# A two-stage expert kernel on one core: the first product in chunks of 384 tokens instead of groups of 288

## The chip, the core and the metric

The kernel runs on one NeuronCore of a Trainium2 chip. The metric is the device time of one execution in microseconds (us); three executions of the kernel before were timed. The engines are PE (TensorE, the matmul array), DVE (VectorE), ACT (ScalarE), POOL (GpSimd) and SP (SyncE, which issues nearly all transfers). PE writes its results into banks of PSUM, of which this kernel names eight: two "A", three "B", one "C", one "M" and one "L".

## What is computed

The reference has three parts, one behind the other. All of it is single precision.

```python
attn_out = linear_attention(q, k, v, omega)       # 2 x 8 heads x 576 tokens x 64
x = attn_out.transpose(0, 2, 1, 3).reshape(1152, 512)
h = x @ w_in                                      # 1152 x 2048   "first product"
g = h / (1 + exp(-1.702 * h))
x = g @ w_out                                     # 1152 x 512    "y"
logits = x @ w_gate                               # 8 experts, capacity 288 tokens each
# top-1 routing; each token goes through its expert's relu(x @ w1) @ w2, times its gate weight
```

## The kernel before, in words

Every product is made of three single-pass matmuls, since an operand is held as a high part and a low part: `mm3` (lines 100 to 103) issues high x high (L101), high x low (L102) and low x high (L103). Small products that are not split run as fp32 in two passes, so that one call leaves two rows in the trace.

The 1152 tokens lie in four groups of GS = 288, G = 0 to 3. The weights of the first product come in NF = 16 blocks m of 128 columns. `do_h(G, m)` makes the first product of group G with block m: four contraction steps of three matmuls, each 288 columns wide, 12 in all; ACT then takes the sigmoid-gelu out of PSUM. For the even groups 0 and 2, ACT does this twice (`ghi`, `g32`) and DVE subtracts (`glo`, L660), and `do_y(G, m)` multiplies the parts by the second weights, again 12 matmuls of 288 columns. The odd groups 1 and 3 never get their y here: only their logits are needed, because a token of an odd group that wins a place in an expert is dealt with in a branch at the end (label "left", L1137 on), which this input does not enter. Their logits come from `g` times `wp`, the second weights already multiplied by the gate (`do_wg`, L520; `do_wp`, L533): `run_lg` collects four such `g` tiles and issues four fp32 matmuls with 8 output rows and 288 columns into one held bank "L" (L705), each in its own column group of the array, so that they run side by side.

The order of work is a list of slots, `seq`: each slot issues one `do_h`, and two slots later `do_consume` (y for even groups, logits for odd ones). In stage one the groups 0, 1 and 3 run over m, group 1 by 3 and group 3 by 5 blocks late; stage two is group 2 alone (16 slots from N2 = 48). Behind it (NSL = 64) stand the two experts, eight slots each, and `do_last`. Side work is hung on slots by number: the decoding of a weight block (`decode`: three DVE operations L260, L263, L266, for the second weights a DVE transpose L270, an ACT cast L276, and a subtraction L277 on POOL), `do_logits`, `do_pos` and `pick_slot`, which chooses an expert and starts its loads. A block is decoded up to six slots ahead of its use (`dlead=6`). The pace is set by `P` in line 16.

`mbank` (L93) hands out PSUM for small results: it alternates between the banks "L" and "M" as long as nothing stands in the list `held`, and gives "M" alone while something does. `do_lg` pops `held` after the last odd block. `do_last` (L937) writes the last group: it brings results back to token order by PE transposes into a bank from `mbank`, and DVE copies from there (`slot_rows` L1045, `chunk` L954; the last column block at L981 to L999). At the very end 76 tiny matmuls (L1009) stand on PE, and one transpose of a cleared tile.

Of the kernel before, what the change touches and what calls it, by code (L numbers as in the profile page):

```python
# [8 lines left out]
F32 = mybir.dt.float32  # L9
# [5 lines left out]
AX = mybir.AxisListType.X  # L15
P = dict(ahead=2, kvlag=2, t2=3, n=5, x=6, dec=(13, 16, 19, 22, 25, 28), tailstep=0.5, zero=26, w0=12, loadlag=10, pv=(0, 4), l1=3, l3=5, db=0.5, hpt=30, dmin=0.9, dc=1, dd=2, dlead=6, dpace=1.5, dv=6)

# [18 lines left out]
def linear_attention__moe__top1_moe_kernel(  # L36
# [26 lines left out]
    TT = 96  # L63
# [556 lines left out]

    L1, L3 = P["l1"], P["l3"]
# [21 lines left out]

    def do_h(G, m, full=False):
        tk = tokens(G)
        hi, lo = w_in(m)
        ps = bank("A", "h_ps")
        for c in range(KD):
            mark["hm"] = mm3(ps[:, :GS], hi[:, c], lo[:, c], x_hi[:, c, :, tk], x_lo[:, c, :, tk],
                             c == 0, c == KD - 1)  # L650
        if G % 2 and not full:
            g1 = gp.tile([128, GS], F32, tag="g1", name="g1", bufs=5)
            mark["a"] = nc.scalar.activation(g1, ps[:, :GS], ACTF.Gelu_apprx_sigmoid)  # L653
            gs[G, m] = g1
            return
        ghi, glo = parts_tile(G != 0)
        nc.scalar.activation(ghi, ps[:, :GS], ACTF.Gelu_apprx_sigmoid)  # L657
        g32 = gp.tile([128, GS], F32, tag="g1", name="g32", bufs=5)
        mark["a"] = nc.scalar.activation(g32, ps[:, :GS], ACTF.Gelu_apprx_sigmoid)  # L659
        mark["v"] = nc.vector.tensor_tensor(glo, g32, ghi.bitcast(F32), ALU.subtract)  # L660
        gs[G, m] = (ghi, glo)

# [17 lines left out]

    def do_lg(G, m):


        i = G - 1 + m % 2
        if i in lgq:
            run_lg()
        lgq[i] = (m, gs.pop((G, m)))
        if len(lgq) == 4 or (G, m) == (3, NF - 1):
            run_lg()
        if (G, m) == (3, NF - 1):  # L690
            held_t.append(gp.tile([128, GS], F32, tag="g1", name="lgt", bufs=5))
            nc.scalar.copy(rows_of(held_t[0]), in_order(held.pop()[:, :GS]))

    lgq, held_t, now = {}, [], [0]

    def run_lg():
        if not held:
            held.append(bank("L", "lgt_ps"))
            nc.vector.memset(held[0][:, :GS], 0.0)
        assert all(m in ready for m, _ in lgq.values()), (lgq, ready)  # L700
# [5 lines left out]
        lgq.clear()  # L706

    def do_consume(G, m):
        (do_lg if G % 2 else do_y)(G, m)

# [38 lines left out]
    def do_logits(G):  # L749
        if G % 2 == 0:  # L750
            ps = mbank("lg_ps")
            for c in range(KD):
                tk = tokens(G)
                nc.tensor.matmul(ps[:2 * E, :GS], wg[:, c].rearrange("p a e -> p (a e)"), x_hi[:, c, :, tk],
                                 start=(c == 0), stop=False)
                nc.tensor.matmul(ps[:E, :GS], wg[:, c, 0], x_lo[:, c, :, tk],
                                 start=False, stop=(c == KD - 1))
            t = gp.tile([2 * E, GS], F32, tag="g1", name="lgy", bufs=5)
            nc.scalar.copy(rows_of(t), in_order(ps[:2 * E, :GS]))
            n = 2 * E  # L760
        else:
            n = 64 if G == 1 else 128
            t = held_t[0]
        ps = mbank("lgr_ps")
        for j in range(TJ):
            nc.tensor.transpose(
                ps[:TT, j * n:(j + 1) * n], t[:n, j * TT:(j + 1) * TT], ident[:n, :n]
            )
        sl = slice(G * TJ, (G + 1) * TJ)
        a0 = 2 * (G == 3)  # L770
        parts = ps[:TT, :TJ * n].rearrange("p (j a e) -> p j e a", j=TJ, e=32 if G % 2 else E)
        nc.vector.tensor_reduce(lg[:, sl], parts[:, :, 0:E, a0:a0 + 2], AX, ALU.add)
        nc.vector.tensor_reduce(mx[:, sl], lg[:, sl], AX, ALU.max)
# [59 lines left out]
    def do_weights():  # L833
        n = NG * TJ
        d = small([TT, n, E], F32, "lgd")
# [101 lines left out]
    def do_last(wt):  # L937
# [65 lines left out]
        gone = gone[0:32, 0:32]  # L1003
        seen = gp.tile([32, 32], F32, tag="g1", name="seen", bufs=5)
# [68 lines left out]
    n0 = at_slot[0, NF - 1] + 3  # L1073
    n3 = at_slot[3, NF - 1] + 3
# [6 lines left out]
    N2 = NSL - NF  # L1081
# [55 lines left out]
    with tc.If(n_left > 0, label="left"):  # L1137
        n_odd = nc.values_load(st["odd"][0:1, 0:1], min_val=0, max_val=NP)
        n_g3 = nc.values_load(st["g3"][0:1, 0:1], min_val=0, max_val=NP)
        with tc.If(n_odd > 0):  # L1140
# [6 lines left out]
            for m in range(NF + 1):  # L1147
                if m < NF:
                    for i in (2 * m, 2 * m + 1):
                        for f in decode(*wseq[i], False):  # L1150
                            f()
                        if i + 3 < len(wseq):
                            load_w(*wseq[i + 3])
                    do_h(1, m, True)
                if m:
                    do_y(1, m - 1)
            with tc.If(n_g3 > 0):
                for m in range(NF + 1):
                    if m < NF:
                        do_h(3, m, True)  # L1160
                    if m:
# [66 lines left out]
```

## Time and profile before

| what | value |
|---|---|
| three executions | 322.84, 321.96, 322.47 us; median 322.47 us |
| the profiled execution | 322.61 us |
| its span in the trace | 320.8 us |
| PE busy | 314.4 us, 98% of the span |
| DVE, ACT, POOL busy | 198.2, 158.6, 45.2 us |
| attention with its tail | up to about 101 us |
| stage one (groups 0, 1, 3) | to about 206 us |
| stage two (group 2) | to about 256 us |
| the two experts and the end | to 320.8 us |

Matmuls are pipelined: the trace shows a 288-column matmul as 0.29 to 0.30 us long, but they start 0.13 us apart. What a matmul costs is therefore read from start to start, and a busy share of 98% does not say that the array works at its peak. The two columns of a timeline row are start and length in us.

### The profile page before, as it was taken

To read this page: it belongs to the slowest core of one execution; us is meant where nothing else is said; L and a number is where in the kernel's file an instruction comes from. 1 tells how busy PE (TensorE), PEld (TensorE's weight loads), DVE (VectorE), ACT (ScalarE), POOL (GpSimd) and SP (SyncE) were. 2 spreads that over 40 slices of the span, in tenths; PEclk is the share of its full clock that TensorE was granted. 3 is DMA by queue.
4 is the path that set the end of the run, shared out by engine and by line. 5 is a ranking of instruction groups with operands and counts; after the bars stand their busy time and mean duration, and the time that the engine had idled before them with its cause. 6 is when DMAs were issued, how large, how long until landed. Compare 5 with 4: busy or idle time off the path is not lost.

```text
span 320.8 us, 7172 instructions
## 1 busy us (share of the span) xinstructions
PE 314.4 (98%) x2844; PEld 301.7 (94%) x2844; DVE 198.2 (62%) x471; ACT 158.6 (49%) x424; POOL 45.2 (14%) x60
## 2 busy tenths in 40 slices
PE   8999999899999999999999999999999999999995
PEld 6999999789999999999999988989999999999995
DVE  5678888988679986686867324036624133567634
ACT  3788888779935434343434342234624233166411
POOL 3111211112000034333433200000000001010000
PEclk9999999999999999999999999999999999999998
DMA  7897672222003655444443000503510000276031
GB/s 210 254 329 176 196 218 65 67 68 66 2 24 109 204 192 167 164 132 133 143 145 109 0 2 2 196 2 131 138 61 3 0 2 0 72 253 200 19 93 44
DMA packets 32132, 35.23 MB, mean 110 GB/s; under 512 B 7553, under 2 KB 27137, under 8 KB 32097
## 3 DMA queue, kind: packets, MB, share of 16 engines
q1 hardware_dynamic: 31808, 34.69, 35.0%
q8 instruction: 23, 0.38, 0.5%
q14 instruction: 13, 0.10, 0.1%
q10 hardware_dynamic: 288, 0.07, 0.1%
HBM read 32.39 MB, written 2.36 MB: 108 GB/s over the span
## 4 chain that ended last, share of the span: by engine, by line
PE 92%; DVE 3%; ACT 1%; DMA 1%; issue 1%; SPq 0%; DVEq 0%; ACTq 0%
PE h_ps L101 14%; PE h_ps L103 13%; PE h_ps L102 13%; PE y L102 8%; PE y L101 8%; PE y L103 8%; PE kvp L367 4%; PE nps L392 4%; PE tp L310 3%; PE pj L101 3%; PE pj L103 2%; PE pj L102 2%; PE t L381 2%; PE lgt_ps L705 1%; PE wg_ps L520 1%; DMA qk_raw<-in_k_dram 1%
## 5 line engine op out<-in xcount | busy, mean ns | idle before, releaser
L660 DVE TENSOR_TENSOR glo<-g,ghi 128x288 fp32r<-128x288 f32 x27 | 13.2, 488 | 44.0 <-ACT g L659 44.0
L266 DVE SCALAR_TENSOR_TENSOR wf<-wraw,wf 128x512 int32<-128x512 int32 x32 | 28.6, 893 | 0.0
L653 ACT ACTIVATE g<-h_ps 128x288 f32<-128x288 f32 x32 | 13.1, 410 | 29.4 <-PE h_ps L103 26.0
L884 DVE TENSOR_TENSOR el<-eraw,eh 128x1024 fp32r<-128x1024 f32 x16 | 19.5, 1225 | 12.8 <-ACT eh L883 12.8
L336 DVE TENSOR_REDUCE nb<-pj 128x4 f32<-128x512 f32 (+1 forms) x40 | 25.1, 627 | 2.5 <-PE pj L103 2.3
L657 ACT ACTIVATE ghi<-h_ps 128x288 fp32r<-128x288 f32 x27 | 11.1, 410 | 28.3 <-PE h_ps L103 28.0
L101 PE MATMUL pj<-om_hi,xh 128*128 128x256 f32 x72 | 24.5, 340 | 0.2 <-ACT qp L349 0.2
L263 DVE SCALAR_TENSOR_TENSOR wf<-wraw,wf 128x512 int32<-128x512 int32 x32 | 23.1, 722 | 0.1
L883 ACT CAST eh<-eraw 128x1024 fp32r<-128x1024 f32 x16 | 16.6, 1046 | 13.0 <-issue 8.3
L349 ACT ACTIVATE qp<-pj,nb 128x128 f32<-128x128 f32 x72 | 21.7, 396 | 0.0
L102 PE MATMUL pj<-om_lo,xh 128*128 128x256 f32 x72 | 21.7, 302 | 0.0
L103 PE MATMUL pj<-om_hi,xl 128*128 128x256 f32 x72 | 21.6, 300 | 0.0
L349 ACT ACTIVATE kp<-pj,nb 128x128 f32<-128x128 f32 x72 | 21.4, 396 | 0.0
L367 PE MATMUL kvp<-vt,kp 128*128 128x65 f32 (+1 forms) x144 | 20.2, 270 | 0.1
L101 PE MATMUL h_ps<-x_hi,win0h 128*128 128x288 f32 x64 | 19.8, 310 | 0.0
L367 PEld LDWEIGHTS kvp<-vt,kp 128*128 128x128 f32 x144 | 18.9, 193 | 0.6 <-ACT kp L349 0.5
L313 ACT CAST xh<-tp 128x256 fp32r<-128x256 f32 (+1 forms) x40 | 14.8, 370 | 9.1 <-PE tp L310 8.9
L103 PE MATMUL h_ps<-x_hi,win0l 128*128 128x288 f32 x64 | 19.2, 300 | 0.1
L101 PE MATMUL h_ps<-x_hi,win1h 128*128 128x288 f32 x64 | 19.3, 301 | 0.0
L101 PE MATMUL h_ps<-x_hi,eh 128*128 128x288 f32 x64 | 19.2, 300 | 0.0
L320 DVE TENSOR_TENSOR xl<-tp,xh 128x256 fp32r<-128x256 f32 (+1 forms) x40 | 15.5, 389 | 5.9 <-ACT xh L313 5.7
L101 PE MATMUL h_ps<-x_hi,win2h 128*128 128x288 f32 x64 | 19.1, 299 | 0.0
(281 smaller groups left out, 1058.9 us busy)
## 6 DMA issues: line engine op xcount, KB each, us to landing
wraw<-in_moe_w_in_dram SPq DMA_DIRECT2D x16, 512.0 KB, 3.7
wraw<-in_moe_w_out_dram SPq DMA_DIRECT2D x16, 512.0 KB, 3.5
eraw<-in_moe_w_dram SPq DMA_DIRECT2D x16, 512.0 KB, 4.2
qk_raw<-in_v_dram SPq DMA_DIRECT2D x4, 512.0 KB, 5.1
qk_raw<-in_q_dram SPq DMA_DIRECT2D x4, 512.0 KB, 5.3
qk_raw<-in_k_dram SPq DMA_DIRECT2D x3, 512.0 KB, 5.3
out_dram<-zer SPq DMA_DIRECT2D x4, 192.0 KB, 4.3
out_dram<-base SPq DMA_DIRECT2D x3, 192.0 KB, 2.1
```

Of the source, the lines that this page charges most:

```text
L101: nc.tensor.matmul(o, lh, rh, start=start, stop=False)
L102: nc.tensor.matmul(o, lh, rl, start=False, stop=False)
L103: return nc.tensor.matmul(o, ll, rh, start=False, stop=stop)
L263: nc.vector.scalar_tensor_tensor(f, high, -0x40000000, f, ALU.bitwise_and, ALU.bitwise_or)
L266: nc.vector.scalar_tensor_tensor(f, low, 29, f, ALU.logical_shift_right, ALU.bitwise_or)
L313: nc.scalar.copy(xh[:, :n], tp[:, :n])
L320: nc.vector.tensor_tensor(xl[:, :n], tp[:, :n], xh[:, :n].bitcast(F32), ALU.subtract)
L336: mark["M", s] = nc.vector.tensor_reduce(nb[:, :nj], pj[:, :nj * M].rearrange("p (a m) -> p a m", m=M), AX, ALU.min)
L349: nc.scalar.activation(t[:, i], pj[:, i * M:(i + 1) * M], ACTF.Exp, bias=nb[:, i:i + 1], scale=-1.0)
L367: nc.tensor.matmul(ps[:, o:o + n], kp[:, i], vts[p][:, u, c0:c0 + n], start=(f == 0), stop=(f == NU - 1))
L883: nc.scalar.copy(hi, tv)
L884: nc.vector.tensor_tensor(lo, tv, hi.bitcast(F32), ALU.subtract)
```

## The change

The first product is cut otherwise. Instead of four groups of 288 there are three chunks of CS = 384 tokens: A is group 0 and the first 96 tokens of group 1, B is group 2 and the first 96 of group 3, C is what is left of the groups 1 and 3 (192 and 192). `do_h(X, m)` issues 12 matmuls of 384 columns. Out of the bank, ACT takes for A and B the two gelus of 288 columns as before and two more of 48 columns each (tile `ga`); for C one gelu of 384 columns (`gc`). The order is A and C interleaved (C four blocks late, `lc=4`) in stage one, and B alone in stage two; there are 48 slots instead of 64.

The logits of odd tokens are collected from these parts. `run_lg` no longer runs when four tiles are there but at given slots, takes the pairs of blocks that are ready, and issues fp32 matmuls of 48 columns (A, B) and 192 columns (C) into three regions of the held bank; `odd_out` copies the regions out. `held` is not popped any more. The logits of group 3 are finished four slots behind stage two. The tile `g1` has one buffer instead of five, decoding runs two to four slots ahead, and the 76 tiny matmuls are gone.

```diff
-P = dict(..., l1=3, l3=5, db=0.5, hpt=30, dmin=0.9, dc=1, dd=2, dlead=6, dpace=1.5, dv=6)
+P = dict(..., lc=4, db=0.5, hpt=30, dmin=0.75, dlead=2, dc=1, dd=1.5, dv=6)
...
+    CS = GS + TT
+    BH = TT // JF // 2
+    CB = (GI - TT // JF) * JF
     seq = []
-    for r in range(NF + L3):
-        seq += [(G, r - l) for G, l in ((0, 0), (1, L1), (3, L3)) if 0 <= r - l < NF]
-    at_slot = {gm: n for n, gm in enumerate(seq)}
-    seq += [(2, m) for m in range(NF)]
+    for r in range(NF + LC):
+        seq += [(X, r - l) for X, l in (("A", 0), ("C", LC)) if 0 <= r - l < NF]
+    at_slot = {xm: n for n, xm in enumerate(seq)}
+    seq += [("B", m) for m in range(NF)]
...
+    def chunk(t, c, X):
+        if X == "C":
+            return t[:, c].rearrange("p j (b i) -> p b j i", b=2)[:, :, :, GI + TT // JF:2 * GI]
+        o = 0 if X == "A" else 2 * GI
+        return t[:, c, :, o:o + CS // JF]
+    def do_h(X, m):
+        hi, lo = w_in(m)
+        ps = bank("A", "h_ps")
+        for c in range(KD):
+            mark["hm"] = mm3(ps[:, :CS], hi[:, c], lo[:, c], chunk(x_hi, c, X), chunk(x_lo, c, X),
                              c == 0, c == KD - 1)
+        if X == "C":
+            g = gp.tile([128, CS], F32, tag="gc", name="gc", bufs=3)
+            mark["a"] = nc.scalar.activation(g, ps[:, :CS], ACTF.Gelu_apprx_sigmoid)
+        else:
+            v = ps[:, :CS].rearrange("p (j i) -> p j i", j=JF)
+            h_parts("ACB".index(X), m, v[:, :, :GI])
+            g = gp.tile([128, TT], F32, tag="ga", name="ga", bufs=6)
+            for b in range(2):
+                nc.scalar.activation(g[:, b * TT // 2:(b + 1) * TT // 2].rearrange("p (j i) -> p j i", j=JF),
+                                     v[:, :, GI + b * BH:GI + (b + 1) * BH], ACTF.Gelu_apprx_sigmoid)
+        lgq.append((now[0], X, m, g))
...
     def run_lg():
         if not held:
             held.append(bank("L", "lgt_ps"))
-        with queued(mark["hm"]):
-            last = gates(sorted(wws), [wgq.pop(0)] if wgq else [])
+        todo = [q for q in lgq if q[0] < now[0] and q[2] in ready]
+        todo = [q for q in todo if any(o[1] == q[1] and o[2] == q[2] ^ 1 for o in todo)]
+        last = mark["hm"]
+        for X in "ACB":
+            at, w = region[X]
+            for b in range(2):
+                for q in todo:
+                    if q[1] != X:
+                        continue
+                    m, i = q[2], 2 * b + q[2] % 2
+                    with queued(last):
+                        nc.tensor.matmul(held[0][32 * i:32 * i + E, at:at + w], wp[:, m], q[3][:, b * w:(b + 1) * w],
+                                         start=((X == "B", i) not in opened), stop=(X != "A" and m >= NF - 2))
+        lgq[:] = [q for q in lgq if not any(q is t for t in todo)]
         with queued(last):
-            for i, (m, g) in sorted(lgq.items()):
-                nc.tensor.matmul(held[0][32 * i:32 * i + E, :GS], wp[:, m], g, start=(m < 2), stop=(m >= NF - 2))
+            gates(sorted(wws), [wgq.pop(0)] if wgq else [])
...
-        end = bank("A", "end_ps")
-        for _ in range(76):
-            tc.keep_in_program_order(nc.tensor.matmul(end[:32, 64:96], ones_bf[:, :32], ones_bf[:, :32], start=True, stop=True))
...
-        need = at_slot[0, m] + (0 if kd == "in" else 2) - P["dlead"]
-        n = max(int(i * P["dmin"]), min(need, int(i * P["dpace"])))
+        n = round(2 * max(i * P["dmin"], i - P["dlead"])) / 2
...
+    for n in [LC, *range(LC + 2, last_a + 1, 4), *range(last_a + 2, N2 + 1, 2)]:
+        slot(n, run_lg)
+    for n in range(N2 + 4, NSL + 1, 4):
+        slot(n, run_lg)
+    slot(N2 + 1, lambda: odd_out("C"))
+    slot(N2 + 1, lambda: odd_out("A"))
+    slot(NSL + 1, lambda: odd_out("B"))
...
-    slot(n3 + 1, lambda: do_logits(3))
+    slot(NSL + 4, lambda: do_logits(3))
```

Three places show what this does to PE's list of instructions.

The first is one of the breaks in stage one at which the gates and the odd logits are computed. Here is PE before (`h_ps` is the first product's bank, `g_2522` and the like are gelu tiles of the groups 1 and 3):

```order
L103 MATMUL h_ps<-x_hi,win2l 128x288
L533 MATMUL wg_ps<-back,ww 32x8 x8
L520 MATMUL wg_ps<-wt,wg_d 32x64 x16
L705 MATMUL lgt_ps<-g_2522,wp 8x288
L705 MATMUL lgt_ps<-g_2632,wp 8x288
L705 MATMUL lgt_ps<-g_2575,wp 8x288
L705 MATMUL lgt_ps<-g_2653,wp 8x288
L101 MATMUL h_ps<-x_hi,win2h 128x288
```

And here is PE in the changed program, at such a break (`ga`: four calls for two blocks of chunk A; `gc`: four for two of C):

```order
L103 MATMUL y_1698<-ghi,wout3l 128x288
L726 MATMUL lgt_ps<-ga,wp 8x48 x4
L726 MATMUL lgt_ps<-gc,wp 8x192 x4
L533 MATMUL wg_ps<-back,ww 32x8 x8
L520 MATMUL wg_ps<-wt,wg_d 32x64 x16
L101 MATMUL h_ps<-x_hi,win2h 128x384
```

The logits now stand ahead of the gate products, as eight narrower calls instead of four, and the first product around them is 384 columns wide. Behind the attention there are ten such breaks before: one with L520 alone, six with all three lines (two logit calls in the first of them, four in the others), one with L533 and logits, two with logits alone (four calls and two). In the changed program there are eleven up to the start of stage two: one with L520 alone, one with L533 and `ga`, one with L520 and `ga`, one with `gc` and both gate lines, four like the piece above, and three with the last logits (with L533; `ga` and `gc`; `gc` alone). Four more are new in stage two.

The second place is stage two, where PE before runs from group 2's first product to its y without a break; in the changed program this stands between them (`y_3058` is the last column block of y):

```order
L103 MATMUL y_3058<-ghi,wout1l 128x288
L726 MATMUL lgt_ps<-ga,wp 8x48 x8
L101 MATMUL h_ps<-x_hi,win2h 128x384
```

Eight calls for four blocks of chunk B stand together, two for each column group.

The third place is `do_last`, the return to token order. Before, PE has the eight transposes of two row blocks in one piece:

```order
L103 MATMUL y_4219<-hhh,el 128x288
L934 MATMUL zt_ps<-ident,z 96x128 x8
L101 MATMUL y_4219<-hhh,eh 128x288
```

In the changed program they stand apart, with seven matmuls of y between the first two fours:

```order
L979 MATMUL zt_ps<-ident,z 96x128 x4
L101 MATMUL y_4147<-hhh,eh 128x288
L102 MATMUL y_4147<-hhl,eh 128x288
L103 MATMUL y_4147<-hhh,el 128x288
L101 MATMUL y_4147<-hhh,eh 128x288
L102 MATMUL y_4147<-hhl,eh 128x288
L103 MATMUL y_4147<-hhh,el 128x288
L101 MATMUL y_4147<-hhh,eh 128x288
L979 MATMUL zt_ps<-ident,z 96x128 x4
```

The last three transposes of the kernel stood in the order of their row blocks before (tiles 4381, 4382, 4383, the first two from `mbank`, the third a bank "A"):

```order
L988 MATMUL zt_ps_4381<-ident_133,z_4216 96x128
L988 MATMUL zt_ps_4382<-ident_133,zl_4384 96x128
L988 MATMUL zt_ps_4383<-ident_133,zl_4385 96x128
L1009 LDWEIGHTS ones_bf_86
```

In the changed program the third block (4311, bank "A") stands ahead of the second (4310, which shares bank "M" with 4309), and no tiny matmuls follow:

```order
L1033 MATMUL zt_ps_4309<-ident_133,z_4144 96x128
L1033 MATMUL zt_ps_4311<-ident_133,zl_4313 96x128
L1033 MATMUL zt_ps_4310<-ident_133,zl_4312 96x128
L1053 MATMUL end_ps_4333<-ident_133,gone_4328 32x32
```

## Rows read from the trace of the kernel before

**Rows 1.** The page: engines over the span, and TensorE's granted clock by slices.
```profile
PE 314.4 (98%) x2844; PEld 301.7 (94%) x2844; DVE 198.2 (62%) x471; ACT 158.6 (49%) x424; POOL 45.2 (14%) x60
PEclk9999999999999999999999999999999999999998
```
**Rows 2.** The page: the chain that ended last, shares by engine.
```profile
PE 92%; DVE 3%; ACT 1%; DMA 1%; issue 1%; SPq 0%; DVEq 0%; ACTq 0%
```
**Rows 3.** Windows, PE: stretch, its us, busy us (instructions), clock, DMA share, GB/s.
```profile
222.48:267.11 44.63, 44.63 (x338) 1.00 0.14 40
```
**Rows 4.** Timeline of PE, attention: second and sixth of six 256-column matmuls, twice.
```profile
60.87 0.28 PE L102 MATMUL pj<-om_lo,xh 128*128 128x256 f32 x1
...
61.34 0.28 PE L103 MATMUL pj<-om_hi,xl 128*128 128x256 f32 x1
...
76.13 0.28 PE L102 MATMUL pj<-om_lo,xh 128*128 128x256 f32 x1
...
76.61 0.28 PE L103 MATMUL pj<-om_hi,xl 128*128 128x256 f32 x1
```
**Rows 5.** Timeline of PE, a full break in stage one.
```profile
171.35 0.29 PE L103 MATMUL h_ps<-x_hi,win2l 128*128 128x288 f32 x1
171.57 0.31 PE L533 MATMUL wg_ps<-back,ww 128*32 128x8 f32 x16
171.72 0.63 PE L520 MATMUL wg_ps<-wt,wg_d 128*32 128x64 f32 x32
172.17 0.67 PE L705 MATMUL lgt_ps<-g,wp 128*8 128x288 f32 x8
...
173.01 0.30 PE L102 MATMUL h_ps<-x_lo,win2h 128*128 128x288 f32 x1
```
**Rows 6.** Timeline of PE, a break with logits alone.
```profile
205.45 0.29 PE L103 MATMUL h_ps<-x_hi,win3l 128*128 128x288 f32 x1
205.67 0.67 PE L705 MATMUL lgt_ps<-g,wp 128*8 128x288 f32 x8
...
206.51 0.30 PE L102 MATMUL h_ps<-x_lo,win0h 128*128 128x288 f32 x1
```
**Rows 7.** Timelines of PE and DVE in do_last: two row blocks transposed and copied.
```profile
301.16 1.04 PE L934 MATMUL zt_ps<-ident,z 128*96 128x128 f32 x8
301.95 0.38 PE L101 MATMUL y<-hhh,eh 128*128 128x288 f32 x1
301.86 1.36 DVE L1050 COPY_PREDICATED base<-p_mk,zt_ps 96x512 f32<-96x512 int32 x2 [0.73 <-PE zt_ps L934]
```
**Rows 8.** Timelines of PE, DVE, ACT and SP's queue over the last column block.
```profile
315.10 0.31 PE L988 MATMUL zt_ps<-ident,z 128*96 128x128 f32 x1 [0.35 <-DVE z L984]
315.68 2.07 PE L1009 MATMUL end_ps<-ones_bf 96*32 96x32 bf16 x76
315.45 0.72 DVE L991 COPY_PREDICATED base<-p_mk,zt_ps 96x128 f32<-96x128 int32 x3
315.84 0.69 ACT L993 ACTIVATE base<-base,gw 96x128 f32<-96x128 f32 x2 [4.16 <-DVE base L991]
316.73 1.11 SPq L999 DMA_DIRECT2D out_dram<-base  x1
```
**Rows 9.** Groups of DVE and POOL in stage one, 119.92 to 185.71 us.
```profile
L266 DVE SCALAR_TENSOR_TENSOR wf<-wraw,wf 128x512 int32<-128x512 int32 x17 | 17.6, 1036 | 0.0
L263 DVE SCALAR_TENSOR_TENSOR wf<-wraw,wf 128x512 int32<-128x512 int32 x17 | 11.6, 683 | 0.0
L260 DVE TENSOR_SCALAR wf<-wraw 128x512 int32<-128x512 int32 x17 | 7.1, 417 | 0.0
L270 DVE STREAM_TRANSPOSE wt<-wf 128x512 f32<-128x512 f32 x9 | 6.3, 704 | 0.0
L660 DVE TENSOR_TENSOR glo<-g,ghi 128x288 fp32r<-128x288 f32 x10 | 5.5, 546 | 21.9 <-ACT g L659 21.9
L277 POOL TENSOR_TENSOR win2l<-wf,win2h 128x512 fp32r<-128x512 f32 x4 | 5.2, 1302 | 5.1 <-ACT win2h L276 5.1
```

More of the change, by code (lines that the diff above doesn't have):

```diff
@@ L642, in parts_tile, with h_parts, do_h_group @@
         return [gp.tile([128, GS], F32R, tag=tag, name=tag, bufs=2) for tag in ("ghi", "glo")]
-    def do_h(G, m, full=False):
+    def chunk(t, c, X):
[3 more added lines that the diff above has]
+        return t[:, c, :, o:o + CS // JF]
+    def h_parts(G, m, v):
+        ghi, glo = parts_tile(G != 0)
+        nc.scalar.activation(ghi.rearrange("p (j i) -> p j i", j=JF), v, ACTF.Gelu_apprx_sigmoid)
+        g32 = gp.tile([128, GS], F32, tag="g1", name="g32", bufs=1)
+        mark["a"] = nc.scalar.activation(g32.rearrange("p (j i) -> p j i", j=JF), v, ACTF.Gelu_apprx_sigmoid)
+        mark["v"] = nc.vector.tensor_tensor(glo, g32, ghi.bitcast(F32), ALU.subtract)
+        gs[G, m] = (ghi, glo)
+    def do_h_group(G, m):
         tk = tokens(G)
@@ L648, in do_h @@
         for c in range(KD):
-            mark["hm"] = mm3(ps[:, :GS], hi[:, c], lo[:, c], x_hi[:, c, :, tk], x_lo[:, c, :, tk],
-                             c == 0, c == KD - 1)
[L651 to L661, printed above, removed]
+            mm3(ps[:, :GS], hi[:, c], lo[:, c], x_hi[:, c, :, tk], x_lo[:, c, :, tk], c == 0, c == KD - 1)
+        h_parts(G, m, ps[:, :GS].rearrange("p (j i) -> p j i", j=JF))
+    def do_h(X, m):
[3 more added lines that the diff above has]
+            mark["hm"] = mm3(ps[:, :CS], hi[:, c], lo[:, c], chunk(x_hi, c, X), chunk(x_lo, c, X),
+                             c == 0, c == KD - 1)
+        if X == "C":
[9 more added lines that the diff above has]
+        lgq.append((now[0], X, m, g))
     def y_banks():
@@ L679, in do_y @@
                 nc.vector.tensor_tensor(x_lo[sl], y, x_hi[sl].bitcast(F32), ALU.subtract)
[L681 to L694, printed above, removed]
+    lgq, odd_t, now = [], [], [0]
+    region = {"C": (0, CB), "A": (CB, TT // 2), "B": (CB + TT // 2, TT // 2)}
+    opened = set()
     def run_lg():
@@ L699, in run_lg, with odd_out, do_consume @@
             nc.vector.memset(held[0][:, :GS], 0.0)
-        assert all(m in ready for m, _ in lgq.values()), (lgq, ready)
-        with queued(mark["hm"]):
-            last = gates(sorted(wws), [wgq.pop(0)] if wgq else [])
-        with queued(last):
-            for i, (m, g) in sorted(lgq.items()):
-                nc.tensor.matmul(held[0][32 * i:32 * i + E, :GS], wp[:, m], g, start=(m < 2), stop=(m >= NF - 2))
-        lgq.clear()
-    def do_consume(G, m):
-        (do_lg if G % 2 else do_y)(G, m)
+        todo = [q for q in lgq if q[0] < now[0] and q[2] in ready]
[11 more added lines that the diff above has]
+                                         start=((X == "B", i) not in opened), stop=(X != "A" and m >= NF - 2))
+                    opened.add((X == "B", i))
+        lgq[:] = [q for q in lgq if not any(q is t for t in todo)]
+        with queued(last):
+            gates(sorted(wws), [wgq.pop(0)] if wgq else [])
+    def odd_out(X):
+        at, w = region[X]
+        ps = held[0][:, at:at + w]
+        if X == "C":
+            odd_t.append(gp.tile([128, CS], F32, tag="gc", name="odd", bufs=3))
+            nc.gpsimd.memset(odd_t[0][:, CB:], 0.0)
+            nc.scalar.copy(rows_of(odd_t[0][:, :CB]), in_order(ps))
+        else:
+            o = CB + (X == "B") * TT
+            for b in range(2):
+                r = slice(64 * b, 64 * b + 64)
+                nc.scalar.copy(rows_of(odd_t[0][r, o + b * w:o + (b + 1) * w]), in_order(ps[r]))
+    def do_consume(X, m):
+        if X != "C":
+            do_y("ACB".index(X), m)
     def hp(f):
@@ L761, in do_logits @@
         else:
-            n = 64 if G == 1 else 128
-            t = held_t[0]
+            n = 128
+            t = odd_t[0]
+        at = [j * TT for j in range(TJ)] if G % 2 == 0 else [CB + (G == 3) * TT, 0, TT]
         ps = mbank("lgr_ps")
@@ L766, in do_logits @@
             nc.tensor.transpose(
-                ps[:TT, j * n:(j + 1) * n], t[:n, j * TT:(j + 1) * TT], ident[:n, :n]
+                ps[:TT, j * n:(j + 1) * n], t[:n, at[j]:at[j] + TT], ident[:n, :n]
             )
         sl = slice(G * TJ, (G + 1) * TJ)
-        a0 = 2 * (G == 3)
         parts = ps[:TT, :TJ * n].rearrange("p (j a e) -> p j e a", j=TJ, e=32 if G % 2 else E)
-        nc.vector.tensor_reduce(lg[:, sl], parts[:, :, 0:E, a0:a0 + 2], AX, ALU.add)
+        if G % 2:
+            a0 = 2 * (G == 3)
+            nc.vector.tensor_reduce(lg[:, G * TJ:G * TJ + 1], parts[:, 0:1, 0:E, :], AX, ALU.add)
+            nc.vector.tensor_reduce(lg[:, G * TJ + 1:(G + 1) * TJ], parts[:, 1:, 0:E, a0:a0 + 2], AX, ALU.add)
+        else:
+            nc.vector.tensor_reduce(lg[:, sl], parts, AX, ALU.add)
         nc.vector.tensor_reduce(mx[:, sl], lg[:, sl], AX, ALU.max)
@@ L834, in do_weights @@
         n = NG * TJ
-        d = small([TT, n, E], F32, "lgd")
+        d = gp.tile([TT, n, E], F32, tag="ga", name="lgd", bufs=6)
         nc.vector.tensor_tensor(d, lg, mx.unsqueeze(2).to_broadcast([TT, n, E]), ALU.subtract)
```

19 lines of the change are left out of this document (10 added, 9 removed).

## The prediction
> **What bounds the kernel now.** I read the page's engine shares first: PE is busy over 98% of the span, DVE over 62%, and the granted clock stands at its upper level of 2.4 GHz from early on to the last slice [rows 1]. The chain that ended last is PE for 92% [rows 2]. Behind the attention, from about 102 us to 315 us, the timeline of PE is unbroken but for two or three waits of a fraction of a microsecond; so in this stretch the time is the sum of what PE has to issue, and an engine beside it counts only if it becomes late. The third view is the start-to-start step, since busy time overlaps itself: in 44.63 us PE starts 28 blocks of 12 matmuls of 288 columns, 336 in all, which is 132.8 ns each [rows 3]. These blocks alternate between the first product, whose moving operand lies in four pieces of 72, and y, whose operand is one piece, and their steps do not differ; how the columns lie in memory is no cost here.
>
> **The first product.** Before, 4 groups x 16 blocks x 12 = 768 matmuls of 288 columns: 768 x 132.8 ns = 102.0 us. After, 3 x 16 x 12 = 576 of 384 columns. The columns are the same, 221,184; what can be gained is only what a matmul costs beside its columns. The trace has no 384-column matmul, so I bound its step. If everything over 288/2.4 = 120 ns is a price per matmul, the step is 132.8 + 96/2.4 = 172.8 ns, and the sum falls by 2.5 us. If the step grows in proportion, it is 177.1 ns and nothing is gained. The nearest other row is the 256-column matmul of the attention: 0.47 and 0.48 us over four steps, 118.8 ns [rows 4]. A line through 256 and 288 columns has 0.44 ns per column and gives 174.9 ns; the reading to 0.01 us leaves some 2 ns of play. I take 175.5 ns, between that line and proportion: 576 x 175.5 = 101.1 us, a gain of **0.9 us** (0 to 2.5).
>
> A rule of the Trainium skill bears on this: the page "TensorE: Matmul & The Clock Gate", section "Back-to-back issue gap", gives an isolated warm matmul N/2.4 + 2.5 ns. By it 288 columns would take 122.5 ns, where the trace has 132.8, and the sum of the first product would fall by 192 x 2.5 ns = 0.5 us. The trace does not agree on the level; the 10 ns that it has more are the open part of the sum above, per matmul or per column.
>
> **The breaks.** When PE leaves the wide single-pass matmuls for the gates or odd logits and comes back, it pays more than the small matmuls. A break with logits alone: 206.51 - 205.45 less two normal steps = 0.79 us [rows 6]. Its eight rows last 0.67 us; a matmul's own latency is about 0.16 us (0.29 long, 0.133 apart), so about 0.5 us is streaming of 288 columns by four calls side by side, and 0.29 us is the price of leaving and coming back. The full break costs 173.01 - 171.35 less two steps = 1.39 us, with 0.15 us for L533 and 0.45 us for L520 [rows 5]. Before: one with L520 alone (0.74), six full (8.34), one with L533 and logits (0.94), two with logits (1.58): 11.6 us. After, four C calls stream 192 columns (0.33 us) and four A calls 48 columns (0.08 us): L520 alone 0.74; L533 with `ga` 0.52; L520 with `ga` 0.82; `gc` with both 1.22; four with all at 1.30, 5.20; the last three 0.85, 0.70 and 0.62; four in stage two, whose eight calls meet twice in each column group, at 0.29 + 0.16, 1.80, of which the first shares its exit with a `do_pos` that stands there anyway (-0.1). Sum 12.4 us, **0.8 us more**. Bounds: with calls of 48 columns nearly free and half the price of leaving, 0; if the 128 rows of the A and B calls did not overlap at all (0.08 us a call, 64 calls, less what is counted), 3.8 us more.
>
> **The held bank.** The code never pops `held` any more, so from stage one on `mbank` gives bank "M" alone. At most places its users depend on each other anyway. At three they don't. In `do_last` PE put eight transposes for two row blocks out in one piece, and DVE copied them in 1.36 us, from 0.70 us behind the first one on [rows 7]. Now the second four need the first copy's end, about 0.70 + 0.74 + 0.05 = 1.49 us behind the first transpose; four transposes (0.40) and seven matmuls of y fill about 1.37 us. PE waits 0.12 us, at two places: **+0.25 us** (0.1 to 0.5). In the last column block the first transpose starts at 315.10, its copy at 315.45, and three copies take 0.72 us, some 0.29 each [rows 8]. The second block's transpose now waits for the first copy (315.74); its own copy follows 0.35 us later, at about 316.12, and ends at 316.41, where the whole trio ended at 316.17. ACT's second scaling, done at 316.53 before (315.84 + 0.69), starts behind this copy and takes about 0.39 us, so it ends at 316.85, and the transfer issued at 316.73 goes out **0.3 us later** (0 to 0.5; the issue itself takes 1.11 us, and may catch up).
>
> **At nothing.** The 76 tiny matmuls run from 315.68 to 317.75, beside the transfer's issue, which ends at 317.84 and whose landing is still to come [rows 8]; that covers them, and without the cover they would be worth 0.1 us. The last odd logits move from stage two to behind it, with the same transposes; DVE's part of them is now issued among the operations that choose the second expert, whose first weights PE awaits soon after; the gelu subtraction that stood there before moves out, so I put 0, with 0.5 us either way. ACT's four small gelus per pair of blocks are hidden while it is busy for half of the span [rows 1]. In the attention's tail PE has the same work in another order: 0, with 0.5 us either way.
>
> **Sum.** -0.9 + 0.8 + 0.25 + 0.3 = +0.45 us on the profiled span of 320.8 us, that is 322.61 + 0.45 = 323.1 us for that execution. It lies 0.14 us above the median of 322.47 us, so I predict **322.9 us**. About 0.3% (1.0 us) is what a measurement of this kernel can tell from no change.
>
> **Rivals.** First, the price is per matmul: the step is near 172.8 ns, the first product gains 2.5 us, and the sum is 322.47 - 2.5 + 1.35 = 321.3 us, 320.5 if the breaks come out cheaper as well. For it: 10 ns of 132.8 belong to no column at 2.4 GHz. Against it: the 256-column row has about as large a share of excess (12 of 118.8), and a price per matmul would put that step at 119.5, not below. The play of the reading leaves this open: 0.25.
>
> Second, slower: the weights come late in stage one. Per block PE then needs 24 x 175.5 + 12 x 132.8 ns and half a break of 1.30, 6.5 us, instead of 48 x 132.8 and half of 1.39, 7.1 us. DVE needs two decodings of 1.036 + 0.683 + 0.417, one transpose 0.704 and one `glo` 0.546, 5.5 us [rows 9]: 85% of the time instead of 78%, and the lead of a block falls from six slots to two. Behind DVE still come the cast and POOL's 1.30 us. If DVE's backlog exceeds one operation (1.04 us) when a gelu is due, PE waits; at 0.25 us in each of 12 blocks that is 3 us: 325.9 us. For it: `g1` with one buffer ties ACT to DVE; against it: DVE has 1.0 us a block to spare, and POOL takes 2.6 of 6.5 us. 0.18.
>
> Third, the small logit calls don't overlap: 3 us more than in my sum, 325.9 us. Against it: eight rows of 288 columns in 0.67 us [rows 6] are overlapped already. 0.07.
>
> **How the numbers follow.** Forecast 0.50: 322.9 us, by itself 321.8 to 324.0; of it 0.03 faster, 0.37 within 0.3% and 0.10 slower. First rival 0.25: 0.20 faster, 0.05 within. Second 0.18 and third 0.07: slower, but for 0.03 of a half-sized loss that stays within. That makes faster 0.23, same 0.45, slower 0.32. The range reaches to 320.9 (most of the first rival) and 325.2 us (weaker forms of the other two).
>
> **What would show it.** The step of the 384-column matmuls in an unbroken block: near 175 ns (forecast), 173 (first rival) or 177. Eleven breaks up to stage two and four in it, of 0.45 to 1.3 us. In stage one no PE wait named after POOL's or DVE's low parts; with them the second rival holds. In `do_last` two waits of PE on DVE, and the last transfer issued 0.3 us further behind the last y than before. The prediction is wrong if the step lies outside 172 to 178 ns, if the breaks cost less than before, or if waits appear in a place that none of this names.

## The result, and the profile after

The changed kernel takes 324.18 us (median of 7 runs, 323.34 to 324.72) against 322.41 us for the kernel before: a ratio of 1.0062 with a 95% interval of 1.0041 to 1.0082 (the two medians alone give 1.0055), so it is slower by 1.3 to 2.6 us. That lies in the range that was given, but outside the likeliest case (within 0.3%). Its profiled execution has a span of 322.3 us, 1.5 us more than the one before.

The page of the changed kernel, engines, granted clock and chain, answers to [rows 1, 2]:

```profile
span 322.3 us, 6948 instructions
PE 313.2 (97%) x2704; PEld 299.4 (93%) x2704; DVE 209.0 (65%) x473; ACT 160.0 (50%) x476; POOL 51.7 (16%) x61
PEclk9999999999999999999999999999999999999999
PE 89%; DVE 5%; ACT 2%; issue 1%; DMA 1%; POOL 1%; SPq 0%; DVEq 0%; ACTq 0%
```

The clock is at its upper level all through. PE's share of the chain has fallen from 92% to 89%, and POOL stands in it. The list of PE's waits between the attention and the end has one line now (waited for, us in total, times, longest); before, it had none:

```profile
PE h_ps L103 <- POOL win1l L277: 1.6, 2, 0.8
```

The timeline around the first of the two, all engines (start, duration):

```profile
118.48 0.62 ACT L276 CAST win1h<-wf 128x512 fp32r<-128x512 f32 x1 [0.30 <-DVE wf L266]
...
119.19 1.49 POOL L277 TENSOR_TENSOR win1l<-wf,win1h 128x512 fp32r<-128x512 f32 x1 [41.09 <-ACT win1h L276]
...
119.55 1.67 DVE L263 SCALAR_TENSOR_TENSOR wf<-wraw,wf 128x512 int32<-128x512 int32 x1
119.61 0.29 PE L102 MATMUL y<-glo,wout1h 128*128 128x288 f32 x1
...
120.73 0.45 PE L103 MATMUL h_ps<-x_hi,win1l 128*128 128x384 f32 x1 [0.82 <-POOL win1l L277]
...
121.01 0.34 PE L101 MATMUL h_ps<-x_hi,win1h 128*128 128x384 f32 x1
```

PE starts a matmul at 119.61 and the next only at 120.73, when POOL's low half of `win1` is done: 0.98 us more than a step. The step behind it is 0.28 instead of 0.17 us, so a wait costs 0.11 us more than it lasts. DVE's decoding operation beside POOL's takes 1.67 us, where its mean before was 0.68 [rows 9]. The second wait, behind the matmul at 126.15, costs 0.91 us:

```profile
125.48 1.71 POOL L277 TENSOR_TENSOR win1l<-wf,win1h 128x512 fp32r<-128x512 f32 x1 [1.28 <-ACT win1h L276]
...
127.24 0.44 PE L103 MATMUL h_ps<-x_hi,win1l 128*128 128x384 f32 x1 [0.75 <-POOL win1l L277]
```

POOL had been idle for 41 us when it began the first of these halves, right behind ACT's cast, so neither a backlog of POOL nor a slowed DVE explains the first wait: the cast came late, and POOL then takes 1.49 us. In the kernel before POOL took even longer for the same half:

```profile
114.27 1.72 POOL L277 TENSOR_TENSOR win1l<-wf,win1h 128x512 fp32r<-128x512 f32 x1 [36.15 <-ACT win1h L276]
```

But there the first matmul that reads it started at 118.51, 2.5 us behind its end, and PE did not wait.

Adding up PE's start-to-start steps of both traces up to the first of the last three transposes (315.10 before, 317.17 after) gives where these 2.07 us come from:

| term | forecast | measured |
|---|---|---|
| columns of the first product | -0.9 | -1.44 |
| breaks for gates and odd logits | +0.8 | +1.10 (11.63 to 12.73) |
| waits for late weights and gelus, with the step behind each | 0 | +2.36 (0.58 to 2.94) |
| transposes of `zt` in `do_last` | +0.25 | +0.28 |
| the rest (not taken apart) | 0 | -0.23 |
| from the last transposes to the span's end | +0.3 | -0.62 (5.73 to 5.11) |

The sum is +1.45 us, the difference of the spans. Two terms are far from the forecast, the waits and the end; most of the experiments are about them.

### The profile page after: what moved, and what is told of

The parts are those of the page before. It is cut to its first block, busy times and chain, and to the rows that moved or that the text cites. A ratio compares the mean times of both kernels' runs of the same rounds, so it can differ in the third digit from the quotient of the medians.

```text
span 322.3 us, 6948 instructions
## 1 busy us (share of the span) xinstructions
PE 313.2 (97%) x2704; PEld 299.4 (93%) x2704; DVE 209.0 (65%) x473; ACT 160.0 (50%) x476; POOL 51.7 (16%) x61
## 3 DMA queue, kind: packets, MB, share of 16 engines
HBM read 32.39 MB, written 2.36 MB: 108 GB/s over the span
## 4 chain that ended last, share of the span: by engine, by line
PE 89%; DVE 5%; ACT 2%; issue 1%; DMA 1%; POOL 1%; SPq 0%; DVEq 0%; ACTq 0%
PE h_ps L101 13%; PE h_ps L103 12%; PE h_ps L102 12%; PE y L102 8%; PE y L103 8%; PE y L101 8%; PE kvp L367 4%; PE nps L392 4%; PE tp L310 3%; PE pj L101 3%; PE pj L102 2%; PE pj L103 2%; PE t L381 2%; PE lgt_ps L726 2%; DVE wf L260 1%
## 5 line engine op out<-in xcount | busy, mean ns | idle before, releaser
L266 DVE SCALAR_TENSOR_TENSOR wf<-wraw,wf 128x512 int32<-128x512 int32 x32 | 35.5, 1111 | 0.6
L659 DVE TENSOR_TENSOR glo<-g,ghi 128x288 fp32r<-128x288 f32 x27 | 12.3, 454 | 21.6 <-ACT g L658 21.6
L263 DVE SCALAR_TENSOR_TENSOR wf<-wraw,wf 128x512 int32<-128x512 int32 x32 | 26.0, 811 | 0.1
L678 ACT ACTIVATE gc<-h_ps 128x384 f32<-128x384 f32 x16 | 7.9, 492 | 27.5 <-PE h_ps L103 25.2
L102 PE MATMUL h_ps<-x_lo,eh 128*128 128x288 f32 x64 | 19.1, 298 | 0.0
L103 PE MATMUL h_ps<-x_hi,el 128*128 128x288 f32 x64 | 18.9, 295 | 0.0
L103 PE MATMUL h_ps<-x_hi,win1l 128*128 128x384 f32 x48 | 16.4, 341 | 1.6 <-POOL win1l L277 1.6
L310 PE MATMUL tp<-ident,qk_raw 128*128 128x128 f32 x72 | 16.2, 294 | 1.2 <-DVE xl L320 0.7
```

The costliest lines, as they stand in the source:

```text
L102: nc.tensor.matmul(o, lh, rl, start=False, stop=False)
L103: return nc.tensor.matmul(o, ll, rh, start=False, stop=stop)
L263: nc.vector.scalar_tensor_tensor(f, high, -0x40000000, f, ALU.bitwise_and, ALU.bitwise_or)
L266: nc.vector.scalar_tensor_tensor(f, low, 29, f, ALU.logical_shift_right, ALU.bitwise_or)
L310: nc.tensor.transpose(tp[:, i * 128:(i + 1) * 128], rows, ident)
```

## The experiments

Times are medians with the ratio to the kernel before, timed beside it on the same chip; the changed kernel stands at 1.0062. In the traces the attention's last product (L392) starts anywhere from 94.0 to 95.9 us, though no edit touches it; so the traces are compared from there on.

**The low halves on DVE: `a_dv10`, `a_dvall`.** In `P`, where `dv` counts the decodings whose low half DVE subtracts:

```
-dv=6)
+dv=10)    # a_dv10
+dv=26)    # a_dvall
```

> The changed kernel with the low halves of four more weight blocks (first-layer and second-layer weights of blocks 6 and 7) subtracted on DVE instead of POOL. In the changed kernel's trace PE stands 0.98 and 0.91 us longer than a step of its own before two matmuls that read such halves of the first-layer weights, and the step behind each wait is 0.11 us long too: 2.1 us. Theory (late weights): POOL takes 1.49 and 1.71 us for these two halves and holds DVE's decoding up beside it (1.67 us for an operation of 0.68); on DVE they take 0.69 us, both waits go, and the time falls by 1.6 to 2.1 us. Rival (DVE is full): four more operations, 2.8 us, on a DVE that is 80% to 90% busy there only move the wait to the decoding behind them or to glo: less than 0.5 us.

`a_dv10`: 321.90 us, 0.9978 (0.9963 to 0.9993), which is 2.3 us under the changed kernel and just faster than the kernel before. The timeline at the same place:

```profile
118.92 0.68 DVE L277 TENSOR_TENSOR win1l<-wf,win1h 128x512 fp32r<-128x512 f32 x1
...
119.53 0.69 DVE L263 SCALAR_TENSOR_TENSOR wf<-wraw,wf 128x512 int32<-128x512 int32 x1
119.64 0.29 PE L103 MATMUL y<-ghi,wout1l 128*128 128x288 f32 x1
119.77 0.34 PE L103 MATMUL h_ps<-x_hi,win1l 128*128 128x384 f32 x1
```

The half is there at 119.60, and PE goes on at its step. The waits fall from 2.94 to 1.06 us, 1.88 less, and the stretch from the attention's last product to the first of the last three transposes is 1.88 us shorter too. So the waits account for all of it; the other 0.5 us by which the two spans differ (322.3 and 319.9) lies ahead, in the attention, which no edit touched. The rival, a DVE that is full, falls.

> The changed kernel with the low halves of all decoded weight blocks on DVE, none on POOL. POOL takes 1.3 us for one and lengthens what DVE does beside it (1.4 to 1.7 us for an operation of 0.68), DVE takes 0.69. If DVE's time beside POOL is lost nearly one for one, DVE is no busier without POOL and the time is that of the run with ten on DVE, 0.998 of before, or a few tenths of a us less (the wait of 0.04 us behind it goes). Rival: DVE's sum, 6.1 us of the 6.6 us that a pair of blocks takes, leaves no room for the order, glo comes late, and PE waits some 0.3 us in each of the later blocks: 2 us more.

`a_dvall`: 321.86 us, 0.9977 (0.9962 to 0.9992). The views of 120 to 180 us: one row for a kernel (length, then busy us and number of instructions of PE, PEld, DVE, ACT, POOL, then clock and DMA). Before:

```profile
120.00:180.00 60.00, 60.00 (x678) 56.94 (x679) 41.92 (x68) 24.55 (x62) 22.03 (x17) 1.00 0.42 133
```

The changed kernel, and its groups of the two longer decoding operations on DVE (count, busy us, mean ns):

```profile
120.00:180.00 60.00, 58.52 (x579) 56.83 (x580) 56.32 (x75) 24.54 (x72) 31.02 (x20) 1.00 0.46 149
...
L266 DVE SCALAR_TENSOR_TENSOR wf<-wraw,wf 128x512 int32<-128x512 int32 x19 | 26.7, 1404 | 0.6
L263 DVE SCALAR_TENSOR_TENSOR wf<-wraw,wf 128x512 int32<-128x512 int32 x19 | 15.7, 828 | 0.0
```

All low halves on DVE:

```profile
120.00:180.00 60.00, 60.00 (x624) 58.26 (x626) 51.89 (x95) 24.63 (x76) 0.00 (x0) 1.00 0.47 147
...
L266 DVE SCALAR_TENSOR_TENSOR wf<-wraw,wf 128x512 int32<-128x512 int32 x19 | 13.1, 687 | 0.2
L263 DVE SCALAR_TENSOR_TENSOR wf<-wraw,wf 128x512 int32<-128x512 int32 x19 | 12.8, 672 | 0.0
```

DVE does 95 operations instead of 75 and is busy 4.4 us less. The mean of L266 is 687 ns without POOL and 1404 ns with POOL busy for half of the time: what POOL takes over costs DVE 16.5 us in these two groups alone. The kernel before showed this already [rows 9]: 1036 ns of L266 there is a mean over both cases, at 22 us of POOL.

**The place of the decoding: `a_lead`, `a_early`.**

```
-dlead=2
+dlead=4                                                                  # a_lead
-n = round(2 * max(i * P["dmin"], i - P["dlead"])) / 2
+n = round(2 * max(i * P["dmin"] - 0.75, i - P["dlead"] - 0.75, 0)) / 2   # a_early
```

> The changed kernel with every decoding of a weight block behind the attention allowed two slots earlier (dlead 4 instead of 2), nothing else. Theory (the lead is short): the two long waits for the low halves of win1 go, and the time falls by 1.6 to 2.1 us, as in the run with the halves on DVE. Rival (the decoding is bound by its engines, not by its place): the operations are put out earlier but DVE, ACT and POOL come no earlier, and the time moves by less than 0.5 us, or rises because decoding is now queued ahead of the attention's tail on DVE.

`a_lead`: 325.65 us, 1.0102 (1.008 to 1.0125), 1.5 us slower than the changed kernel. The theory as put was a misreading of the code: with `dmin` of 0.75 the first nine decodings stay where they were, so both waits for `win1` stay (steps of 1.11 and 1.08 us). The later decodings lie closer together, and DVE beside POOL doesn't follow; new waits appear, the longest a step of 0.80 us at 141.94 for a late `glo`, and the waits come to 4.69 us in all.

> The changed kernel with every decoding behind the attention moved forward by one slot, from the ninth on (the earlier ones by 0.5 to 1 slot, the first not), low halves on POOL as in the changed kernel. The run with a longer lead did not test that: it left the first nine decodings where they were, so both waits for win1 stayed (1.11 and 1.08 us), and it packed the later ones closer. A slot is 1.7 to 2.1 us of PE. Theory (place): the halves of win1 come a slot earlier, both waits go, 1.6 to 2.1 us less than the changed kernel. Rival (rate): DVE with POOL beside it cannot decode faster, it is busy 56.3 of 60 us there, so the order put out earlier is worked off no earlier: less than 0.7 us.

`a_early`: 323.20 us, 1.0026 (1.0011 to 1.0042). Both waits for `win1` are gone, with POOL's slow halves in place: the waits fall to 1.23 us. So an earlier start cures them too, and the rival, that DVE's rate is the limit, falls; they came from a start that is too late for a slow engine. The gain is nearly halved because the first gates now come from 100.3 us on, right behind the attention's tail, instead of at 104.1, and PE works them off in three stops instead of one: breaks cost 0.76 us more. And DVE is late for `glo` at two places, as here (PE's timeline):

```profile
165.88 0.29 PE L101 MATMUL y<-ghi,wout3h 128*128 128x288 f32 x1
166.46 0.40 PE L102 MATMUL y<-glo,wout3h 128*128 128x288 f32 x1 [0.29 <-DVE glo L659]
```

**The held bank: `a_bank`, `a_dvbank`, `a_dvallbank`.**

```
 slot(NSL + 1, lambda: odd_out("B"))
+slot(NSL + 1, held.clear)
```

> The changed kernel with the list of the held bank emptied behind the last copy of odd logits, so that the small products alternate between two banks again. Theory: in do_last the two excess steps of PE (0.13 and 0.07 us, with 0.1 behind them) go, and in the last block the three copies take 0.72 us again instead of 1.00, so that the last transfer goes out 0.2 us earlier: 0.4 us less in all. Rival: those waits are covered by what the end waits for anyway: below 0.1 us.

`a_bank`: 323.46 us, 1.0031 (1.0019 to 1.0043): 0.7 us less by the medians, and by the ratios 0.2 to 1.8. In its trace the eight transposes of `do_last` go out in one piece again, the last three copies take 0.72 us, and the last transfer is issued 1.63 us behind the first transpose instead of 1.81:

```profile
303.82 1.03 PE L979 MATMUL zt_ps<-ident,z 128*96 128x128 f32 x8
...
317.77 0.31 PE L1033 MATMUL zt_ps<-ident,z 128*96 128x128 f32 x1 [0.35 <-DVE z L1029]
...
318.12 0.72 DVE L1036 COPY_PREDICATED base<-p_mk,zt_ps 96x128 f32<-96x128 int32 x3
...
319.40 0.34 SPq L1044 DMA_DIRECT2D out_dram<-base  x1
```

The trace accounts for 0.3 us on PE and 0.1 to 0.2 at the end, the 0.4 that was expected; what the medians show above that is within their play. (In this trace the attention's last product starts 0.9 us later than in the changed kernel's, so its span, 322.8 us, shows no gain.)

> The changed kernel with both edits: four more low halves of weights on DVE, and two banks again for the small products behind stage two. The two edits touch different places, so their effects should add: from the traces 1.9 us of waits and 0.5 us around the two late transposes, 2.4 us under the changed kernel, that is a ratio to the kernel before of 0.995 to 0.998. Rival (what is taken away in stage one is waited for again further on, for the second expert's weights): no faster than with the halves on DVE alone, 0.998.

> The changed kernel with two edits: all low halves on DVE, two banks again for the small products behind stage two. If the two add as they did with ten halves on DVE: 0.996 of the kernel before, 321.3 us; the difference from the run with three edits is what the earlier decoding is worth.

`a_dvbank`: 321.49 us, 0.9962 (0.9943 to 0.9980); `a_dvallbank`: 321.40 us, 0.9967 (0.9949 to 0.9985). Both beat both kernels, by 0.6 to 1.8 us over the kernel before for the first. That the bank's part adds to DVE's is in the traces: from the attention's last product to the first of the last three transposes the changed kernel takes 222.14 us, `a_dv10` 1.88 less, `a_bank` 0.28 less and `a_dvbank` 2.17 less. The intervals are too wide to show it in the times.

> The changed kernel with three edits: all low halves on DVE, decodings one slot earlier, two banks again for the small products behind stage two. What is left to gain over all halves on DVE is 0.5 us of late weights and gelus between 105 and 126 us and 0.5 us at the end: ratio to the kernel before 0.994 to 0.996 (320.6 to 321.2 us). Rival (decoding ahead of the attention's tail on DVE makes that tail late): 0.998 or more.

`a_best` (`dv=26`, the earlier decoding and the bank): 321.60 us, 0.9975 (0.9961 to 0.9988). The expected 0.994 to 0.996 is missed. The waits are down to 0.33 us, but the two extra stops of PE cost 0.76 us: earlier decoding pays nothing on top.

**A break left out: `a_nolgb`.**

```
-for n in range(N2 + 4, NSL + 1, 4):
-    slot(n, run_lg)
```

> The changed kernel without the four stops of stage two in which PE computes the odd logits of the last chunk (this leaves those logits out: they stay zero, so the tokens' choice of an expert is another). In the trace they take 0.46, 0.50, 0.50 and 0.49 us of PE: entry, eight products, transition back. Theory (PE's time is a sum): the time falls by 1.9 us against the changed kernel, ratio about 1.000. Rival (stage two has slack that another wait fills, or the choice of other experts moves the end): less than 1 us.

The whole run took 526.93 us, since with these logits at zero the tokens go to other experts and the work for what is left over starts; its time answers nothing. Its trace up to the first expert does. From the first y of stage two to the first product of the expert, with and without the three stops that lie in it:

```profile
205.35:257.01 51.66, 51.66 (x379) 50.91 (x379) 18.01 (x36) 20.50 (x64) 0.00 (x0) 1.00 0.21 67
```
```profile
205.06:255.27 50.21, 50.21 (x332) 50.20 (x331) 18.01 (x36) 20.49 (x64) 0.00 (x0) 1.00 0.22 69
```

1.45 us less; the three stops cost 0.46 + 0.50 + 0.50 by their own steps. There PE's time is a plain sum.

**The tiny matmuls: `b_notiny`, `b_notiny2`, `a_tiny`.** Taken out of the kernel before, and put back into the changed one:

```
 end = bank("A", "end_ps")
-for _ in range(76):
-    tc.keep_in_program_order(nc.tensor.matmul(end[:32, 64:96], ones_bf[:, :32], ones_bf[:, :32], start=True, stop=True))
```

> The kernel before without the 76 tiny matmuls at its end, nothing else. Forecast on record: they cost nothing, 0 to 0.1 us. Rival, from the two traces: from the first of the last three transposes to the span's end it is 5.7 us with them and 5.1 us without, though the last transfer is issued 0.2 us later; the last issue takes 1.11 us with them and 0.32 us without. If they hold the issue up, the time falls by 0.6 to 0.8 us.

> The changed kernel with the 76 tiny matmuls back at its end. The kernel before became slower by 1.4 us without them (0.6 to 2.1), with a granted clock that fell before the end in most of its runs (means of 0.992 to 0.995 against 0.996 to 1.000); the changed kernel has no such matmuls, and its means are 0.996 to 1.000. Theory (they hold the clock up at the end, which here it is anyway): no change from the changed kernel, within 0.6 us. Rival (the changed kernel has lost by their removal too): 0.8 to 1.5 us faster than the changed kernel.

> The kernel before without the 76 tiny matmuls again, for a second look at its end: it was slower by 0.6 to 2.1 us, but the one profile taken of it was among its fastest executions and showed a tail of 5.6 us, as with them. If the loss is at the end, a slower execution shows a longer tail (6.5 us or more behind the first of the last three transposes) or a granted clock that falls before these transposes; if it is a matter of when the first expert's and second expert's weights land, PE waits longer near 283 us (0.57 us in the first look, 0.16 with the tiny matmuls).

The kernel before without them: 323.83 us, 1.0047 (1.0026 to 1.0067), and again 324.49 us, 1.0057 (1.0034 to 1.008). The changed kernel with them: 325.42 us, 1.0092 (1.0068 to 1.0116), slower than without. The first two expectations missed: taking them out of the one costs 1.4 and 2.0 us by the medians (0.8 to 2.6 by the intervals), putting them into the other costs 1.2 us by the medians (0 to 2 by the ratios, so at the edge of what can be told). The third held: the loss is at the end. From the first of the last three transposes to the span's end it is 7.89 us in the trace of `b_notiny2`, an execution of 324.9 us, against 5.73 before and 5.66 in that of `b_notiny` (322.84 us); in the changed kernel it is 6.18 us with them against 5.11. What differs is PE's last branch (its sequencer's instructions by line: count, duration in ns). Before:

```profile
L1137 PEldq COMPARE_BRANCH  x1: 1381/1381/1381, 317.6 to 317.6; - x1
```

`b_notiny2`, with SP's wait there:

```profile
L1135 PEldq COMPARE_BRANCH  x1: 3887/3887/3887, 317.7 to 317.7; - x1
...
SPq L1221 <- PEq L1135: 2.9, 1, 2.9
```

The changed kernel, and the changed kernel with them:

```profile
L1187 PEldq COMPARE_BRANCH  x1: 388/388/388, 319.8 to 319.8; - x1
```
```profile
L1189 PEldq COMPARE_BRANCH  x1: 1921/1921/1921, 319.5 to 319.5; - x1
```

The branch takes 0.39 us in the changed kernel and in all its variants without tiny matmuls, 1.35 to 3.89 us in the others, and where it takes longest SP waits 2.9 us for it. The second part is SP's last issue: 1.11 us before [rows 8], 0.32 after:

```profile
318.98 0.32 SPq L1044 DMA_DIRECT2D out_dram<-base  x1
```

Before, a transfer of instructions falls into it, by the DMA of 316.2 to 317.9 us:

```profile
q1 hardware_dynamic: 112, 0.05, 13.1%
q8 instruction: 1, 0.02, 4.6%
```

In `b_notiny2` no instruction transfer lies there, and the issue takes 0.34 us. Taken together, the 13 traces other than that of `a_nolgb` give one picture. In eleven the span ends 2.97 to 3.02 us behind the end of SP's last issue; in the two with the longest branches (`b_notiny2`, `a_tiny`) it ends 1.49 us behind the end of the branch. Each of the four long branches ends 1.4 to 1.5 us behind the end of a 16 KB transfer of instructions on queue q8, and each of the two long issues (before and `b_notiny`) 0.4 us behind one; in the nine traces with the short branch none ended within 13 us ahead of the branch's end. So the end hangs on where these transfers fall. That this is the cause is an inference from which traces go together: no run moved such a transfer alone, and why the tiny matmuls move it to the good in one kernel and to the bad in the other stays open. The granted clock is not the cause: in `a_dvall` and `a_best` it stood at 0.50, the lower level (1.2 GHz), for the whole of the branch, and this took 0.39 us all the same.

## Why the prediction was half right

**Columns: right in kind, too small.** The forecast step was 175.5 ns. 24 matmuls of stage one, from one block's first to the next y:

```profile
137.64 0.34 PE L101 MATMUL h_ps<-x_hi,win1h 128*128 128x384 f32 x1
...
141.80 0.29 PE L101 MATMUL y<-ghi,wout2h 128*128 128x288 f32 x1
```

That is 173.3 ns; in stage two, with only the last chunk, it is 176, and over all 174.3. So 576 x 174.3 = 100.4 us against 768 x 132.6 = 101.8. With 118.8 ns at 256 columns the three sizes lie on one line: 0.434 ns a column and 7.5 ns a matmul. The first rival's price (132.8 - 120 = 12.8 ns a matmul) was too high; the forecast's, 4.7 ns by a step of 175.5, too low: I had moved the line's 174.9 towards proportion without a row for it. The 3 ns between the stages are unexplained. By the rule of the Trainium skill that the prediction cites (page "TensorE: Matmul & The Clock Gate", section "Back-to-back issue gap", 2.5 ns a matmul) the gain would be 0.5 us, an estimate. The trace does not agree: it shows 7.5 ns a matmul, and 1.44 us.

**Breaks: right.** +1.10 us for 0.8. The full break is 1.31 us here (143.48 to 144.87, less a step, and with 0.09 us ahead) for 1.30 forecast; those in stage two took 0.46 to 0.50 for 0.45:

```profile
143.48 0.27 PE L726 MATMUL lgt_ps<-ga,wp 128*8 128x48 f32 x8
143.57 0.51 PE L726 MATMUL lgt_ps<-gc,wp 128*8 128x192 f32 x8
143.90 0.29 PE L533 MATMUL wg_ps<-back,ww 128*32 128x8 f32 x16
144.02 0.63 PE L520 MATMUL wg_ps<-wt,wg_d 128*32 128x64 f32 x32
144.58 0.45 PE L101 MATMUL h_ps<-x_hi,win1h 128*128 128x384 f32 x1
144.87 0.34 PE L102 MATMUL h_ps<-x_lo,win1h 128*128 128x384 f32 x1
```

Eight rows of 48 columns take 0.09 us, so the third rival falls: the small calls overlap.

**The held bank: right.** PE waits twice in `do_last`, 0.28 us with the steps behind, for 0.25 [rows 7]; the first wait is half of the time between these two rows:

```profile
304.18 0.29 PE L101 MATMUL y<-hhh,eh 128*128 128x288 f32 x1
304.44 0.64 PE L979 MATMUL zt_ps<-ident,z 128*96 128x128 f32 x4
```

At the end the second block's transpose waits for the first copy as forecast, and the last issue starts 0.18 us later, for 0.3 [rows 8].

**Late weights: the step that failed.** I gave them no term, and 0.18 to a rival of 3 us. The rival's cause is the one that decided, at another size and place: not 0.25 us in each of 12 blocks, but two waits of 1 us for the third and fourth block of `win1`, and small ones, 2.36 us more than before in all. By the prediction's own sign (a PE wait in stage one named after POOL's low parts) the second rival holds. What spoke against it was a rate, DVE with 5.5 of 6.5 us a block, and a rate was the wrong thing to ask for. As a rate it was low, since it took DVE's durations of before as fixed [rows 9]: they were means over a POOL that worked a third of the time, and with POOL at half the time L266 went from 1036 to 1404 ns and DVE to 56.3 of 60 us. Yet DVE kept up, and behind 127.5 us no low half of `win` or `wout` was late any more. What failed is the lead: these two are the first low halves of `win` that POOL makes behind the attention, with the cast done only 0.1 and 0.6 us before the block that needs it starts, and 1.49 and 1.71 us of POOL do not fit in. The point that a block's lead falls from six slots to two was in the text, and could have given the place. Both sides of this were tested: a faster engine for these halves (`a_dv10`) and an earlier start with POOL still at work (`a_early`) each make the two waits go. The first product itself did gain: with the two causes of delay taken out (`a_dvbank`, `a_dvallbank`) the changed kernel is 0.5 to 1.8 us faster than the kernel before. The kernel before with its low halves on DVE was not run.

**At nothing: wrong for the end.** The end became 0.62 us shorter, not 0.3 longer: SP's last issue starts 0.18 us later behind the first of the last three transposes, but ends 0.62 us earlier, because it takes 0.32 us and not 1.11 (the prediction had the 1.11 and noted that the issue may catch up). That the missing tiny matmuls did this is not shown: without them the kernel before kept its long issue in one trace and got a longer branch in the other. The attention's tail, ACT's small gelus and the moved logits cost nothing visible (-0.23 us with everything else).

**The time: in the range partly by luck.** The sum was +0.45 us and the spans differ by 1.45. The waits alone were missed by 2.36 us; the columns, the end and the rest, each better than forecast, took 1.7 us of that back, and the upper end of the range came from weaker forms of the second and third rival.

## What to carry to other kernels

Where two engines slow each other, a duration from the trace holds only for the share of time in which the other one worked; before giving such an engine more work, split the group by that (here a mean of 0.69 us without the other engine and 1.4 us with it), and ask whether the helper saves anything. When a change shortens the lead of a producer, look first at the first items that it makes, not at the mean over all blocks. A time at the very end of a kernel that changes by half a microsecond or more may go with where a transfer of instructions falls, and then says little about the edit next to it.

## What the runs showed of the hardware

- DVE's 512-element decoding operation takes 0.67 to 0.69 us on average with POOL idle (`a_dvall`) and up to 1.70 us beside POOL's subtraction (changed kernel, stage one), which itself takes 1.30 to 1.86 us for what DVE does in 0.69.
- A step of PE behind a wait is 0.11 us longer than its own (both waits for `win1`).
- Single-pass matmuls behind one another start 118.8, 132.6 and 174.3 ns apart at 256, 288 and 384 columns, at a granted clock of 1.00 (upper level).
- PE's last branch took 0.39 us in nine traces and 1.35 to 3.89 us in the four in which a 16 KB transfer of instructions ended 1.4 to 1.5 us ahead of the branch's end; SP's last issue took 0.32 to 0.34 us, and 1.06 and 1.11 us in the two traces in which such a transfer lay in it.
